# Three slots of 128 partitions in place of four of 72 for the coarse half of attention, in a one-core attention and two-layer kernel

## The chip, the cores and the metric

The kernel runs on one core of a Trainium2 chip. The time is that of the device in microseconds (us), from the start of the program to its end. TensorE multiplies (PE in the rows; its weight loads are PEld), VectorE is DVE, ScalarE is ACT, GpSimd is POOL, and SyncE (SP) issues most transfers. TensorE's results land in eight PSUM banks, and DVE or ACT copies them out.

## The reference

There are 4 batches of 8 heads with 576 positions of 64 numbers. Each head is attended to twice, and the results are added:

```
q_d, k_d, v_d = means of 4 neighbouring positions     # 144 rows each
out_up    = repeat(softmax(q_d k_d^T / 8) v_d, 4)     # the coarse half
out_local = softmax(q k^T / 8 where |i - j| < 4) v    # the local half
x = (out_up + out_local) as 2304 x 512
x = (h * sigmoid(1.702 h)) w_out,  h = x w_in         # layer 1, 512 -> 2048 -> 512
x = elu(h2) w2_out,                h2 = x w2_in       # layer 2
```

The change is in the coarse half alone.

## The kernel before

**Units.** Attention is worked through in units of two heads (head 0 on partitions 0 to 63, head 1 on 64 to 127 of the transposed q and k). There are 16 units: four early ones of batch 0 (whose second half of positions follows in four late ones that have no coarse half of their own), and twelve later ones, "packed", two of which are under way at a time.

**The coarse half of a unit.** `down_products` (step QD) multiplies coarse q by coarse k: the 144 queries of a head are cut into two halves of 72, so there are four slots [72 queries, 144 keys], two for each head, in two PSUM banks. Step ND takes the largest of each row (DVE), NS scales it, EC makes four exps with their sums (ACT, L637), MP weighs them (DVE). `pdt_piece` (PD, L693) turns each slot with two 72x72 transposes, eight in all, into two banks, and PC copies each bank to SBUF (ACT, L701). `pv_down_products` (PVD, L727 and L1023) multiplies them by the coarse v, `vd`, with 72 keys at a time; DN copies the sum. `vd` is made on POOL (L481, L483) from two loads of v (L471), one for each head.

**The local half.** The scores of the windows (QK, L566 and L960), masks, maxima and exps, then `pt_first` and `pt_last` turn the weights (L999, four and one transposes of 128x128), and the products with v (PV, L748 and L1051) follow.

**Shapes on TensorE.** A matmul occupies a part of the 128x128 array that follows from its rows (the contraction) and its columns (the stationary operand's): the layers' matmuls and all the transposes before take 128x128, QD 64x128, PVD 128x64, QK and the packed PV 64x64. In a shape smaller than the array, matmuls on different parts run beside each other: QD's two heads (rows 0 to 63 and 64 to 127), PVD's two heads, four windows in QK and PV. A product of plain float32 shows as two records.

**What sets the order.** Up to the middle of layer 1 a list by hand, `OPENING`, gives the order on all engines, token by token (`QD0.e1`: the coarse products of head 0 of early unit 1; `r` are the packed units). In it stand 40 matmuls on ones (`*10`, `*2`, ...: `keep_busy`) whose results nobody reads. Behind it, a planner cuts each unit into pieces (`pieces`): `attend` is called twice for each step's h (layer 1, first product, L1225) and twice for each step's y (second product, L1292), and takes the next piece once the pause of the one before is over. The pauses are `LEAD` (before the scores, the coarse scores and the turning of q and k) and `BACK` (the pieces behind the exps). TensorE's order is as written; the other engines' follow from it. The last eight units are worked through in this way. Layer 1's loops over the blocks of tokens and layer 2 (L1418, L1467) are as before.

Of the kernel before, what the change touches and what calls it, by code (L numbers as in the profile page):

```python
# [8 lines left out]
F32 = mybir.dt.float32  # L9
# [9 lines left out]
P = 128  # L19
D = 64  # L20
S = 576
SD = 144
HALF = 72
# [37 lines left out]
    Tk0.e1 Tq0.e1 Ck0.e1 VD0.e0 Tk1.e1 Tq1.e1 Ck1.e1 VD0.e2 QD0.e0 Cq0.e1 VD1.e1 Tq0.e3 Sk.e1 QD1.e0 Cq1.e1 LW.2 ND0.e0  # L61
    Cq0.e3 VD0.e1 Tq1.e3 QK.e0 ND1.e0 VD0.e3 Cq1.e3 NS.e0 Sq.e1 VW.e0 EC.e0 NM.e0 *2 QD0.e1 Sq.e3 EW.e0 ND0.e1 *1 QD1.e1
    LQ.r0 Tk0.e3 GA1.e0 ND1.e1 Tk1.e3 Ck0.e3 W.e0 QK.e1 LW.3 NS.e1 Ck1.e3 MS.e0 VD1.e2 EC.e1 Tk0.e2 LK.r0 Sk.e3 NM.e1
    A1.0 MP.e0 *6 QD0.e3 VD1.e3 EW.e1 VW.e1 Tk1.e2 D1.0 D2.0 PT.e0 ND0.e3 QD1.e3 Ck0.e2 PTC.e0 Tq0.e2 Ck1.e2 ND1.e3
    VW.e3 *1 Tq1.e2 A1.1 QK.l0 W.e1 GA0.e0 NS.e3 Cq1.e2 MS.e1 MP.e1 Cq0.e2 PD0.e0 EC.e3 LW.4 *1 QK.e2 LW.5 GA0.e2 NM.l0
    VW.e2 Sq.e2 EW.l0 *2 PD1.e0 QK.e3 NM.e2 LW.6 GA1.e1 PC1.e0 *1 QK.l1 PC0.e0 NM.e3 A3.0 Sk.e2 EW.e2 PD0.e1 PVD.e0 D3.0
    GA0.e1 EW.e3 *2 PV.e0 W.l0 NM.l1 QD0.e2 VW.l0 MS.l0 DN.e0 EW.l1 QD1.e2 W.e3 GA0.e3 X.e0 D1.1 D2.1 VD0.r0 PC0.e1
    MS.e3 *3 Tq0.r0 A3.1 MP.e3 LW.7 PD1.e1 PT.e1 A1.2 GA1.e2 ND0.e2 PD0.e3 XH.00 Cq0.r0 ND1.e2 A1.3 D3.1 *4 Tk0.r0
    PC0.e3 Ck0.r0 NS.e2 XL.00 *1 PTb.l0 GA1.e3 PTC.e1 EC.e2 Tk1.r0 H.0.0 D1.2 D2.2 PTCb.l0 *1 PD1.e3 W.e2 PT.e3 PC1.e1
    D1.3 D2.3 PC1.e3 Tq1.r0 Ck1.r0 PVD.e1 MP.e2 LQ.r1 A3.3 PV.e1 MS.e2 DN.e1 Cq1.r0 PD0.e2 PTC.e3 PT.e2 LW.8 A3.2 X.e1  # L70
    PD1.e2 PC0.e2 PTc.l0 PV.e3 PC1.e2 PTCc.l0 XH.01 W.l1 PVD.e2 A1.4 D3.2 QK.l2 A1.5 PTC.e2 DN.e2 D3.3 *2 PV.e2 XL.01 *1
    H.0.1 X.e2 D1.4 D2.4 PVD.e3 DN.e3 XH.02 MS.l1 *1 PV.l0 X.e3 GA0.r0 XL.02 VW.l1 XH.03 NM.l2 A1.6 H.0.2 VD1.r0 *1 A3.4
# [24 lines left out]
    D3.28 Y.11.0 A1.31 LQ.r4 VD0.r4 A3.30 MP.r3 PVb.r2 H.15.0 Xa.r2 D1.31 GA0.r4 Xb.r2 VD1.r4 GA1.r4 Y.11.1 H.15.1
    PD0.r3 PD1.r3 D3.30 D2.31 Y.12.0 GL.13 ST.14 VD0.r5 MS.r3 PC0.r3 A3.29 PC1.r3 D3.29 TH.15 PTa.r3 PVD.r3 PVa.r3 A3.31
    PTCb.r3 ST.15 DN.r3 GA0.r5 D3.31 PTCa.r3 Y.12.1 GH.15 GL.15 VW.r3 VD1.r5 PVb.r3 GH.14 Xa.r3 GL.14 Xb.r3 GA1.r5
    Y.13.0 Y.13.1 VW.r4  # L100
# [8 lines left out]
BACK = (2, 2, 2)  # L109
# [16 lines left out]
def kernel(  # L126
# [50 lines left out]
    nc.gpsimd.memset(sumset, 1.0)  # L177

# [212 lines left out]
    class Unit:  # L391
# [73 lines left out]
        def load_half(self, j):  # L465
            tag = ("gh", "gl", "gh", "g")[self.hp] if j == 0 else ("gh", "gl", "gl", "g")[self.hp]
            if self in early:
                r = gpool.tile([HALF, 2, 4, D], F32, tag=tag, name=f"vr{j}_{self.n}", bufs=2 if tag == "g" else None)
            else:
                r = att.tile([HALF, 2, 4, D], F32, tag="vr", name=f"vr{j}_{self.n}")  # L470
            nc.sync.dma_start(  # L471
                out=r.rearrange("g c r d -> g c (r d)"),
                in_=v[self.b, 2 * self.hp + j].rearrange("(c g r) d -> g c (r d)", g=HALF, r=4),
            )
            self.halves[j] = r

        def add_half(self, j):
            if self.vd is None:
                self.vd = self.t([HALF, 2, 2, D], "vd", bufs=2)
            r, vd = self.halves.pop(j), self.vd[:, :, j, :]  # L480
            nc.gpsimd.tensor_tensor(out=vd, in0=r[:, :, 0, :], in1=r[:, :, 1, :], op=ALU.add)  # L481
            for i in (2, 3):
                nc.gpsimd.tensor_tensor(out=vd, in0=vd, in1=r[:, :, i, :], op=ALU.add)  # L483
# [111 lines left out]
        def qk_down(self, j):  # L595
            self.down_products(j)
            self.down_max(j)
            if j == 1:
                self.down_scale()

        def down_products(self, j):
            if j == 0:
                self.nmd = self.t([HALF, 4], "nmd", bufs=4)
                self.pd = self.t([HALF, 4, SD], "pd", bufs=2)
                self.psd = {}
            r = slice(64 * j, 64 * j + 64)
            ps = self.ps([HALF, 2, SD], f"qkd{j}")
# [5 lines left out]
            self.psd[j] = ps  # L613

        def down_max(self, j):
            nc.vector.tensor_reduce(
                out=self.nmd[:, 2 * j:2 * j + 2], in_=self.psd[j], axis=AX.X, op=ALU.max, negate=True
            )
# [16 lines left out]
        def exp_down(self):  # L635
            for i in range(4):
                nc.scalar.activation(  # L637
                    out=self.pd[:, i, :], in_=self.psd[i // 2][:, i % 2, :], func=AF.Exp, bias=self.nmd[:, i:i + 1],
                    scale=self.scale_down(), accum_out=self.sums()[:HALF, self.nslot + i:self.nslot + i + 1],
                )  # L640
# [971 lines left out]
```

## Time and profile before

| | |
|---|---|
| median of 3 runs | 917.64 us (916.98 to 923.25) |
| the profiled execution | 917.48 us, of which the span between its first and last instruction is 915.6 us |
| granted TensorE clock | 1.000, the level of 2.4 GHz |
| busy in the span | PE 905.8 us, DVE 463.1 us, ACT 441.4 us, POOL 60.3 us |
| chain that ended last | PE 91%, DVE 3%, ACT 2%, DMA 2%, the rest 2% |

A row of a timeline gives an instruction's start, its duration, and how many like it follow (`x8`); durations of matmuls overlap, so what one costs is the distance between two starts. A row of the groups gives busy time, the mean of one, and the idle time in front with what ended it.

### The profile page before, as it was taken

How to read it: one execution, taken by the hardware profiler on the slowest of the kernel's cores; microseconds unless marked ns; L12 is line 12 of the kernel's file. 1: busy time of each engine (PE TensorE's matmuls, PEld its weight loads, DVE VectorE, ACT ScalarE, POOL GpSimd, SP SyncE). 2: the span in 40 equal slices, each digit the busy share in tenths (PEclk: the TensorE clock that was granted, in tenths of full speed). 3: DMA queues.
4: the chain of work that ended last, by engine and by line, in shares of the span. 5: the costliest groups of instructions: out<-in, count | busy, mean ns of one | idle time of the engine just before them, and what ended most of it. 6: DMA issues, size and time to landing. Idle time of an engine off the chain costs nothing.

```text
span 915.6 us, 14862 instructions
## 1 busy us (share of the span) xinstructions
PE 905.8 (99%) x5823; PEld 747.3 (82%) x5823; DVE 463.1 (51%) x884; ACT 441.4 (48%) x1119; POOL 60.3 (7%) x126
## 2 busy tenths in 40 slices
PE   9999999999999999999999999999999999999998
PEld 5688977777777788888899888778888888888897
DVE  5999888866667532322237765642233223322232
ACT  6888866444446422422246766643334334333343
POOL 4411112111111100000000000000000000000000
PEclk9999999999999999999999999999999999999999
DMA  9997652432233000100069810020001000100010
GB/s 199 217 238 194 189 132 52 102 62 55 54 64 97 23 15 1 47 1 1 0 206 376 292 47 1 0 93 1 1 12 69 1 1 12 46 1 1 7 40 24
DMA packets 113717, 68.05 MB, mean 74 GB/s; under 512 B 81136, under 2 KB 103152, under 8 KB 113648
## 3 DMA queue, kind: packets, MB, share of 16 engines
q1 hardware_dynamic: 111280, 66.52, 26.7%
q10 hardware_dynamic: 2368, 0.59, 0.4%
q8 instruction: 46, 0.75, 0.3%
q14 instruction: 23, 0.19, 0.1%
HBM read 57.65 MB, written 9.44 MB: 73 GB/s over the span
## 4 chain that ended last, share of the span: by engine, by line
PE 91%; DVE 3%; ACT 2%; DMA 2%; SPq 1%; issue 1%; DVEq 0%
PE h L1418 22%; PE o L1467 22%; PE h L1225 18%; PE y L1292 17%; PE y_both L1292 4%; PE h_both L1225 3%; DMA vw<-in_v_dram 1%; PE pv L1051 1%; PE qk L960 1%; PE ptr L999 1%; PE pdt L693 1%; PE qkd L609 1%; SPq L454 1%; DMA rawq<-in_q_dram 1%; PE pv L1023 1%
## 5 line engine op out<-in xcount | busy, mean ns | idle before, releaser
L1467 PE MATMUL o<-whl2o,g2h 128*128 128x512 f32 x576 | 179.7, 392 | 0.0
L1418 PE MATMUL h<-x2h,whl2i 128*128 128x512 f32 (+1 forms) x640 | 158.9, 370 | 0.0
L1292 PE MATMUL y<-g1h,whl1o 128*128 128x512 f32 (+1 forms) x512 | 152.2, 368 | 0.5 <-ACT ye_both L1306 0.5
L1428 DVE SCALAR_TENSOR_TENSOR g<-e,h 128x512 f32<-128x512 f32 (+1 forms) x80 | 50.7, 634 | 196.8 <-ACT e L1426 196.6
L1225 PE MATMUL h<-xh,whl1i 128*128 128x512 f32 (+1 forms) x640 | 145.2, 352 | 0.1
L1418 PEld LDWEIGHTS h<-x2h,whl2i 128*128 128x128 f32 x640 | 114.6, 188 | 22.6
L1467 PEld LDWEIGHTS o<-whl2o,g2h 128*128 128x128 f32 x576 | 106.9, 188 | 24.1 <-DVE whl2o L239 1.2
L1425 ACT ACTIVATE e<-h 128x512 f32<-128x512 f32 (+1 forms) x80 | 44.6, 557 | 164.6 <-PE h L1418 164.4
L1225 PEld LDWEIGHTS h<-xh,whl1i 128*128 128x128 f32 x640 | 105.4, 189 | 15.5 <-issue 0.4
L1467 PE MATMUL o<-whl2o,g2l 128*128 128x512 f32 x288 | 112.6, 391 | 0.0
L1234 ACT ACTIVATE g<-h 128x512 f32<-128x512 f32 x64 | 38.2, 597 | 142.2 <-PE h L1225 141.8
L1292 PEld LDWEIGHTS y<-g1h,whl1o 128*128 128x128 f32 x512 | 92.6, 189 | 17.4 <-issue 1.3
L1238 DVE SCALAR_TENSOR_TENSOR g<-g,h 128x512 f32<-128x512 f32 x64 | 43.9, 686 | 116.7 <-ACT g L1234 116.7
L1292 PE MATMUL y<-g1l,whl1o 128*128 128x512 f32 (+1 forms) x256 | 93.0, 363 | 0.0
L1418 PE MATMUL h<-x2l,whl2i 128*128 128x512 f32 (+1 forms) x320 | 80.0, 371 | 0.0
L1225 PE MATMUL h<-xl,whl1i 128*128 128x512 f32 (+1 forms) x320 | 73.4, 348 | 0.1
L1435 DVE TENSOR_TENSOR g2l<-g,g2h 128x512 fp32r<-128x512 f32 (+1 forms) x80 | 51.0, 638 | 36.8 <-ACT g2h L1433 22.3
L1433 ACT ACTIVATE g2h<-g 128x512 fp32r<-128x512 f32 (+1 forms) x80 | 47.2, 590 | 43.6 <-DVE g L1428 43.6
L1418 PEld LDWEIGHTS h<-x2l,whl2i 128*128 128x128 f32 x320 | 56.8, 188 | 11.0
L1467 PEld LDWEIGHTS o<-whl2o,g2l 128*128 128x128 f32 x288 | 54.1, 188 | 11.6
L1225 PEld LDWEIGHTS h<-xl,whl1i 128*128 128x128 f32 x320 | 54.1, 189 | 8.2 <-DVE xl L384 0.3
L1251 DVE TENSOR_TENSOR g1l<-g,g1h 128x512 fp32r<-128x512 f32 x64 | 44.0, 687 | 30.1 <-ACT g1h L1244 29.7
(142 smaller groups left out, 1170.8 us busy)
## 6 DMA issues: line engine op xcount, KB each, us to landing
wst1i<-in_moe_w_in_dram SPq DMA_DIRECT2D x16, 512.0 KB
wst1o<-in_moe_w_out_dram SPq DMA_DIRECT2D x16, 512.0 KB
wst2o<-in_moe_w_out_dram SPq DMA_DIRECT2D x16, 512.0 KB
wst2i<-in_moe_w_in_dram SPq DMA_DIRECT2D x16, 512.0 KB
vr<-in_v_dram SPq DMA_DIRECT2D x32, 144.0 KB
out_dram<-ot SPq DMA_DIRECT2D x18, 256.0 KB
y<-ydram SPq DMA_DIRECT2D x16, 256.0 KB
ydram<-ye SPq DMA_DIRECT2D x14, 256.0 KB
```

Source lines behind the costliest of these rows:

```text
L454: queue.dma_start(out=r[:, :, j, :], in_=src[self.b, 2 * self.hp + j].rearrange("(p t) d -> p t d", t=6))
L1225: nc.tensor.matmul(out=hps[blk, fs][:, i, :], lhsT=w_in(1, f, c, wp), rhs=columns(xp, c), start=(n == 0), stop=(n >= len(todo) - nf), skip ...
L1234: return nc.scalar.activation(out=g, in_=hps[blk, fs], func=AF.Tanh, scale=0.851)
L1238: return nc.vector.scalar_tensor_tensor(out=g, in0=g, scalar=1.0, in1=ph, op0=ALU.add, op1=ALU.mult)
L1251: return nc.vector.tensor_tensor(out=gl, in0=g, in1=gh.bitcast(F32), op=ALU.subtract)
L1292: nc.tensor.matmul(out=sums(m), lhsT=w_out(1, f, wp)[:, m, :], rhs=gp[:, i, :], start=(opens and n == 0 and m % per == 0), stop=(last and ...
L1418: nc.tensor.matmul(out=ph[:, :n], lhsT=w_in(2, f, c, wp), rhs=xp[:, c, :n], start=(i == 0), stop=(i == 3 * NK - 1),)
L1425: nc.scalar.activation(out=e[:, :n], in_=ph[:, :n], func=AF.Relu, scale=-1.0)
L1428: urgent["dve"] = nc.vector.scalar_tensor_tensor(out=g[:, :n], in0=e[:, :n], scalar=-1.0, in1=ph[:, :n], op0=ALU.add, op1=ALU.max)
L1433: nc.scalar.activation(out=gh[:, :n], in_=g[:, :n], func=AF.Copy)
L1435: return lambda: nc.vector.tensor_tensor(out=gl[:, :n], in0=g[:, :n], in1=gh[:, :n].bitcast(F32), op=ALU.subtract)
L1467: nc.tensor.matmul(out=ops[bi][i], lhsT=gp[:, i * P:(i + 1) * P], rhs=wo[wp], start=(f == 0 and m == 0), stop=(f == NF - 1 and m == 2),)
```

## The change

A unit's coarse half lies in three slots of 128 partitions. Slots 0 and 1 hold queries 0 to 127 of head 0 and head 1; slot 2 holds queries 80 to 143 of head 0 on partitions 0 to 63 and of head 1 on 64 to 127. Queries 80 to 127 are in two slots, and the transposes take them from one. In slot 2, head 1's keys stand with keys 80 to 143 first.

QD is five products (two of 64x128, three of 64x64 with 64 queries each), ND two reductions over three slots, EC three exps, MP one multiplication over 432 numbers in place of 576. PD is one bank: three transposes of 80 queries, one of slot 2's first 128 columns, then one 64x64 transpose for head 0 and, for head 1, one 64x64 product with the identity. PC is one copy of 432 columns. PVD is one product per head over keys 0 to 79 and one for both heads over the last 64 keys of each, whose stationary operand `tails` holds the two heads' tails of v on its diagonal blocks and zeros elsewhere. v is loaded as 80 keys of both heads and, on 128 partitions, a tail; POOL makes seven additions for a unit in place of six, and sets `tails` to zero at the start.

Steps `QD0 QD1`, `ND0 ND1`, `PD0 PD1` and `PC0 PC1` become one each; in `OPENING` they stand mostly where the second of the two stood, with small moves around them. In the planner's last eight units PD joins the turning of the first four pairs (`turned_over`), and `pt_last` moves from there to the front of `pv`, into the second bank of the products. `BACK` has two pauses in place of three.

```diff
-BACK = (2, 2, 2)
+BACK = (2, 2)
...
+    tails = cpool.tile([P, NHP, P], F32, tag="tails", name="tails")
+    nc.gpsimd.memset(tails, 0.0)
...
+            first = self.ps([P, 2, SD], "qkd0")
+            second = self.ps([P, 1, SD], "qkd1")
+            self.psd = first, second
+            every, last = slice(0, SD), slice(KEYS, SD)
+            for out, j, queries, keys in (
+                (first[:, 0, :], 0, slice(0, P), every), (second[:, 0, :], 1, slice(0, P), every),
+                (first[:TAIL, 1, :], 0, last, every), (first[TAIL:, 1, :KEYS], 1, last, slice(TAIL, SD)),
+                (first[TAIL:, 1, KEYS:], 1, last, slice(0, TAIL)),
+            ):
+                r = slice(64 * j, 64 * j + 64)
                 nc.tensor.matmul(
-                    out=ps[:, c, :], lhsT=self.qkd[0][r, c * HALF:(c + 1) * HALF], rhs=self.qkd[1][r, :],
-                    start=True, stop=True,
-                )
+                    out=out, lhsT=self.qkd[0][r, queries], rhs=self.qkd[1][r, keys], start=True, stop=True,
+                    skip_group_check=True,
+                )
...
-            for i in range(4):
+            for i in range(NDOWN):
...
-        def pdt_piece(self, j):
-            if j == 0:
-                self.pdT = self.t([HALF, 4, SD], "pdT")
-            ps = self.ps([HALF, 2, SD], f"pdt{j}")
-            for kc in range(2):
-                for c in range(2):
+        def pdt_piece(self):
+            self.pdT = self.t([P, 3 * SD], "pdT")
+            ps = self.ps([P, 3 * SD], "pdt")
+            pd = self.pd.rearrange("p s k -> p (s k)")
+            for j, k0 in enumerate((0, SD + TAIL, KEYS)):
+                nc.tensor.transpose(
+                    out=ps[:, SD * j:SD * j + KEYS], in_=pd[:KEYS, k0:k0 + P], identity=ident[:KEYS, :KEYS]
+                )
+            nc.tensor.transpose(
+                out=ps[:, :2 * SD].rearrange("p (j q) -> p j q", j=2)[:, :, KEYS:], in_=pd[:, 2 * SD:2 * SD + P],
+                identity=ident,
+            )
+            last = slice(3 * SD - TAIL, 3 * SD)
+            nc.tensor.transpose(out=ps[:TAIL, last], in_=pd[:TAIL, last], identity=ident[:TAIL, :TAIL])
+            nc.tensor.matmul(
+                out=ps[TAIL:, last], lhsT=pd[TAIL:, last], rhs=ident[TAIL:, TAIL:], start=True, stop=True,
+                skip_group_check=True,
+            )
...
+        def pv_down_into(self, ps):
+            for j in range(2):
+                nc.tensor.matmul(
+                    out=ps[64 * j:64 * j + 64, :], lhsT=self.vd[:, j, :], rhs=self.pdT[:KEYS, SD * j:SD * j + SD],
+                    start=True, stop=False, skip_group_check=True,
+                )
+            nc.tensor.matmul(
+                out=ps, lhsT=self.vtail, rhs=self.pdT[:, 2 * SD:], start=False, stop=True, skip_group_check=True
+            )
...
         def turned_over(self):
             while not self.weighed:
                 deferred.pop(0)()
-            last = self.pt_last()
+            down = self.pdt_piece()
             first = self.pt_first()
+            self.pdt_copy(down)
             self.pt_first_copy(first)
-            self.pt_last_copy(last)
...
         def pv(self):
-            down, banks = self.banks_pv()
-            self.pv_down_products(down)
+            down, last, banks = self.banks_pv()
+            self.turn_slots(last.unsqueeze(1), NPAIR - 1, NPAIR)
+            self.pt_last_copy(last)
+            self.pv_down_into(down)
             self.pv_products(banks)
```

TensorE's queue at the coarse scores of one of the planner's units (batch 2, heads 2 and 3), before and then in the change; the shape is the result's:

```order
L1225 MATMUL h_2_3_2831<-xh_2586,whl1i_757 128x512 x4
L609 MATMUL qkd_2_1_0_2853<-kd_1_0_2711,qd_1_0_2709 72x144 x2
L609 MATMUL qkd_2_1_0_2857<-kd_1_0_2711,qd_1_0_2709 72x144 x2
L1292 MATMUL y_2_2786<-g1h_1_2762,whl1o_1050 128x512
```

```order
L1261 MATMUL h_2_3_2803<-xh_2558,whl1i_749 128x512 x4
L642 MATMUL qkd_2_1_0_2825<-kd_1_0_2683,qd_1_0_2681 128x144
L642 MATMUL qkd_2_1_0_2826<-kd_1_0_2683,qd_1_0_2681 128x144
L642 MATMUL qkd_2_1_0_2825<-kd_1_0_2683,qd_1_0_2681 64x144
L642 MATMUL qkd_2_1_0_2825<-kd_1_0_2683,qd_1_0_2681 64x80
L642 MATMUL qkd_2_1_0_2825<-kd_1_0_2683,qd_1_0_2681 64x64
L1328 MATMUL y_2_2758<-g1h_1_2734,whl1o_1037 128x512
```

The two heads' pairs of products became one for each head over 128 queries and three over 64.

TensorE's queue where the first of these units is turned (`pdt`), before and in the change:

```order
L1225 MATMUL h_2_4_2903<-xh_2586,whl1i_905 128x512 x4
L693 MATMUL pdt_2_0_0_2931<-ident,pd_0_0_2680 72x72 x4
L693 MATMUL pdt_2_0_0_2937<-ident,pd_0_0_2680 72x72 x4
L1292 MATMUL y_2_2786<-g1h_2_2782,whl1o_1229 128x512
```

```order
L1261 MATMUL h_2_4_2875<-xh_2558,whl1i_875 128x512 x4
L725 MATMUL pdt_0_0_2903<-ident,pd_0_0_2652 128x80 x3
L728 MATMUL pdt_0_0_2903<-ident,pd_0_0_2652 128x2x64
L733 MATMUL pdt_0_0_2903<-ident,pd_0_0_2652 64x64
L735 MATMUL pdt_0_0_2903<-ident,pd_0_0_2652 64x64
L1042 MATMUL ptr_2_0_0_2911<-ident,sl_0_0_2598 128x128 x4
L1328 MATMUL y_2_2758<-g1h_2_2754,whl1o_1216 128x512
```

The four transposes of the windows' weights (`ptr`) now stand behind the coarse ones, without layer 1's matmuls between.

Its queue at the products with v of the same unit (`PT`, `vw` and `vd` are its operands), before and in the change:

```order
L1292 MATMUL y_2_2789<-g1h_2_2782,whl1o_1229 128x512
L999 MATMUL ptr_2_0_0_2955<-ident,sl_0_0_2626 128x128
L999 MATMUL ptr_2_0_0_2958<-ident,sl_0_0_2626 128x128 x4
L1225 MATMUL h_2_5_2965<-xh_2586,whl1i_946 128x512 x4
L1225 MATMUL h_2_5_2965<-xl_2587,whl1i_946 128x512 x4
L1225 MATMUL h_2_5_2965<-xh_2586,whl1i_946 128x512 x4
L1023 MATMUL pv_2_0_0_2985<-pdT_0_0_2930,vd_0_0_2431 64x144 x4
L1051 MATMUL pv_2_0_0_2985<-PT_0_0_2957,vw_0_0_2576 64x60
L1051 MATMUL pv_2_0_0_2986<-PT_0_0_2957,vw_0_0_2576 64x57
```

```order
L1328 MATMUL y_2_2761<-g1h_2_2754,whl1o_1216 128x512
L1042 MATMUL pv_2_0_0_2931<-ident,sl_0_0_2598 128x128
L769 MATMUL pv_2_0_0_2930<-pdT_0_0_2902,vd_0_0_2406 64x144 x2
L773 MATMUL pv_2_0_0_2930<-pdT_0_0_2902,tails 128x144
L1085 MATMUL pv_2_0_0_2930<-PT_0_0_2910,vw_0_0_2548 64x60
L1085 MATMUL pv_2_0_0_2931<-PT_0_0_2910,vw_0_0_2548 64x57
L1085 MATMUL pv_2_0_0_2930<-PT_0_0_2910,vw_0_0_2548 64x60
```

The last transpose stood twelve matmuls of layer 1 ahead of the products; now nothing of layer 1 stands between, and `pv_2_0_0_2931`, into which it goes, is the bank of every second product.

ScalarE's queue around the copy of that transpose (`PT`), before and in the change:

```order
L1234 ACTIVATE g_2_4_2923<-h_2_4_2903 128x512
L701 ACTIVATE pdT_0_0_2930<-pdt_2_0_0_2931 72x288
L701 ACTIVATE pdT_0_0_2930<-pdt_2_0_0_2937 72x288
L1244 ACTIVATE g1h_4_2926<-g_2_4_2923 128x512
L1018 ACTIVATE PT_0_0_2957<-ptr_2_0_0_2955 128x128
L1234 ACTIVATE g_2_5_2978<-h_2_5_2965 128x512
L1244 ACTIVATE g1h_5_2981<-g_2_5_2978 128x512
```

```order
L1270 ACTIVATE g_2_4_2895<-h_2_4_2875 128x512
L742 ACTIVATE pdT_0_0_2902<-pdt_0_0_2903 128x432
L1280 ACTIVATE g1h_4_2898<-g_2_4_2895 128x512
L1061 ACTIVATE PT_0_0_2910<-pv_2_0_0_2931 128x128
L780 ACTIVATE dn_0_0_2957<-pv_2_0_0_2930 128x144
L1270 ACTIVATE g_2_5_2997<-h_2_5_2984 128x512
```

Two copies of the coarse transposes became one; the copy of the last pair stands behind the same `g1h`.

## Rows read from the trace of the kernel before

**Rows 1.** The page: busy us of each engine, share of the span, instructions.

```profile
PE 905.8 (99%) x5823; PEld 747.3 (82%) x5823; DVE 463.1 (51%) x884; ACT 441.4 (48%) x1119; POOL 60.3 (7%) x126
```

**Rows 2.** Waits of TensorE: who waited for whom, us in total, times, longest.

```profile
PE pdt L693 <- ACT whl1i L235: 0.7, 2, 0.4
PE pdt L693 <- DVE pd L672: 0.7, 1, 0.7
...
PE pdt L693 <- ACT pdT L701: 0.3, 1, 0.3
```

**Rows 3.** Stretches: length, busy us PE, PEld, DVE, ACT, POOL; clock, DMA share, GB/s.

```profile
12.00:45.00 33.00, 31.36 (x380) 22.64 (x381) 30.06 (x69) 30.15 (x122) 13.96 (x24) 1.00 1.02 219
45.00:100.00 55.00, 53.68 (x562) 48.66 (x558) 52.76 (x116) 43.58 (x128) 7.59 (x12) 1.00 0.85 221
206.00:332.00 126.00, 126.00 (x1057) 99.80 (x1057) 75.96 (x163) 60.96 (x238) 13.67 (x30) 1.00 0.26 56
```

**Rows 4.** Timeline of PE at a unit's coarse scores.

```profile
204.94 1.07 PE L1225 MATMUL h<-xh,whl1i 128*128 128x512 f32 x4
205.94 0.72 PE L609 MATMUL qkd<-kd,qd 64*72 64x144 f32 x8
206.59 0.50 PE L1292 MATMUL y<-g1h,whl1o 128*128 128x512 f32 x1
206.93 0.40 PE L1292 MATMUL y<-g1l,whl1o 128*128 128x512 f32 x1
```

**Rows 5.** Timeline of PE at a unit's coarse transposes.

```profile
275.12 0.40 PE L1292 MATMUL y<-g1h,whl1o 128*128 128x512 f32 x1
275.35 0.66 PE L693 MATMUL pdt<-ident,pd 72*72 72x72 f32 x8
275.82 0.48 PE L1292 MATMUL y<-g1h,whl1o 128*128 128x512 f32 x1
276.14 0.39 PE L1292 MATMUL y<-g1l,whl1o 128*128 128x512 f32 x1
```

**Rows 6.** Timeline of PE at a unit's products with v.

```profile
303.12 0.71 PE L1023 MATMUL pv<-pdT,vd 72*64 72x144 f32 x8
303.76 0.91 PE L1051 MATMUL pv<-PT,vw 64*64 64x60 f32 x40
```

**Rows 7.** Timeline of PE at the first early unit.

```profile
10.96 0.71 PE L609 MATMUL qkd<-kd,qd 64*72 64x144 f32 x4
11.60 0.47 PE L513 MATMUL pt<-ident,rawq 96*128 96x96 f32 x3
12.00 0.71 PE L609 MATMUL qkd<-kd,qd 64*72 64x144 f32 x4
12.64 0.47 PE L513 MATMUL pt<-ident,rawq 96*128 96x96 f32 x3
...
13.15 0.71 PE L566 MATMUL qk<-kT,qT 64*64 64x70 f32 x16
```

**Rows 8.** Groups of all PE's instructions, by form.

```profile
L693 PE MATMUL pdt<-ident,pd 72*72 72x72 f32 x128 | 11.6, 227 | 1.6 <-ACT whl1i L235 0.7 <-DVE pd L672 0.7 <-ACT pdT L701 0.3
...
L999 PE MATMUL ptr<-ident,sl 128*128 128x128 f32 x60 | 9.0, 274 | 0.0
```

**Rows 9.** Groups of ACT's instructions, by form.

```profile
L637 ACT ACTIVATE pd<-qkd,nmd 72x144 f32<-72x144 f32 x64 | 23.2, 379 | 6.7 <-DVE nmd L621 6.7
...
L701 ACT ACTIVATE pdT<-pdt 72x288 f32<-72x288 f32 x32 | 11.8, 416 | 5.4 <-PE pdt L693 5.4
```

**Rows 10.** Timeline of ACT at the planner's first unit.

```profile
212.43 0.60 ACT L1234 ACTIVATE g<-h 128x512 f32<-128x512 f32 x1 [0.44 <-PE h L1225]
...
214.63 0.63 ACT L1244 ACTIVATE g1h<-g 128x512 fp32r<-128x512 f32 x1 [1.01 <-DVE g L1238]
215.79 0.28 ACT L1018 ACTIVATE PT<-ptr 128x128 f32<-128x128 f32 x1 [0.52 <-PE ptr L999]
```

More of the change, by code (lines that the diff above doesn't have):

```diff
@@ L22 @@
 SD = 144
-HALF = 72
+KEYS = 80
+TAIL = 64
+NDOWN = 3
 NWIN = 9
@@ L469, in load_half @@
             else:
[L470 to L473, printed above, removed]
-            )
[L475 to L483, printed above, removed]
+                r = att.tile([P, 2, 4, D], F32, tag="vr", name=f"vr{part}_{self.n}")
@@ new lines, in load_half, with add_half @@
+            self.halves[part] = r
+        def add_half(self, part):
+            r = self.halves.pop(part)
+            if part == 0:
+                self.vd = self.t([KEYS, 2, D], "vd", bufs=2)
+                nc.gpsimd.tensor_tensor(out=self.vd, in0=r[:KEYS, :, 0, :], in1=r[:KEYS, :, 1, :], op=ALU.add)
+                for i in (2, 3):
+                    nc.gpsimd.tensor_tensor(out=self.vd, in0=self.vd, in1=r[:KEYS, :, i, :], op=ALU.add)
+                return
+            t = r[:, 0]
+            for i in (1, 2):
+                nc.gpsimd.tensor_tensor(out=t[:, 0], in0=t[:, 0], in1=t[:, i], op=ALU.add)
+            self.vtail = tails[:, whole.index(self) % NHP]
+            for j in range(2):
+                rows = slice(TAIL * j, TAIL * j + TAIL)
+                nc.gpsimd.tensor_tensor(out=self.vtail[rows, rows], in0=t[rows, 0], in1=t[rows, 3], op=ALU.add)
@@ L808, in one @@
                 self.exp_windows(*{"": qk_at[""], "a": (0, 3), "b": (3, 6), "c": (6, NWIN)}[part])
[L809 to L816 removed]
+            elif step == "PD":
+                ps["pd"] = self.pdt_piece()
+            elif step == "PC":
+                self.pdt_copy(ps.pop("pd"))
             elif kind == "PT":
@@ L948, in banks_pv @@
             first = self.ps([P, n + SD], "pv0")
-            second = self.ps([P, 87, 4], "pv1")
-            return first[:, n:], [first[:, :n].rearrange("p (g r) -> p g r", r=4), second]
+            second = self.ps([P, n + P], "pv1")
+            return first[:, n:], second[:, n:], [t[:, :n].rearrange("p (g r) -> p g r", r=4) for t in (first, second)]
         def qk_products(self):
@@ L1018, in pt_last_copy @@
             nc.scalar.activation(out=self.PT[:, NPAIR - 1], in_=ps[:, :P], func=AF.Copy)
-        def pv_down_products(self, ps):
-            for kc in range(2):
-                for j in range(2):
-                    nc.tensor.matmul(
-                        out=ps[64 * j:64 * j + 64, :], lhsT=self.vd[:, kc, j, :],
-                        rhs=self.pdT[:, 2 * j + kc, :], start=(kc == 0), stop=(kc == 1), skip_group_check=True,
-                    )
-            return ps
         def turned_over(self):
```

179 lines of the change are left out of this document (83 added, 96 removed).

## The prediction

> **What bounds the kernel now.** I read the page first: TensorE is busy for 905.8 of 915.6 us, the others for half of it or less [rows 1]. Then TensorE's own waits: they are few and short, those at the coarse transposes come to 1.7 us [rows 2]. Then the stretches: from 206 us on, where the planner works, TensorE is busy all the time, while DVE is at 60% and ACT at 48%; before that, from 12 to 45 us, all three are near full, ACT for 30.15 and DVE for 30.06 of 33 us [rows 3]. So the time is the length of TensorE's queue, and an instruction less on ACT or DVE is worth only the wait of TensorE that it ends, in the opening alone. In the opening the matmuls on ones stand in the queue as before; they are not shortened by anything that the change does. The question is what the new pieces cost on TensorE, so I went on to its timeline around each step.
>
> **Prices.** One of the layers' matmuls of 512 columns follows the next after 0.23 us (275.12 to 275.35, [rows 5]). Eight transposes of 72 columns last 0.66, the last of them 0.23 [rows 5, 8], so they begin 0.062 apart: 0.86 ns a column. That makes 0.123 for a pass of 144 columns, 0.110 for 128, 0.069 for 80, 0.055 for 64. A plain product has two passes, its two records.
>
> A change of shape costs more than any of these. At the coarse scores the last of the four h matmuls began at 204.94 + 1.07 - 0.39 = 205.62; QD follows 0.32 later, 0.09 over the 0.23; QD's four passes (the two heads beside each other) are 0.49, and the next matmul begins 0.65 after it, 0.16 over; the one behind comes after 0.34, 0.11 over [rows 4]. Going in and coming out is 0.36 together. Between two small shapes, PVD's 128x64 and PV's 64x64, it is 0.64 - 0.49 = 0.15 [rows 6]. So I count 0.15 for a change, and 0.21 where a matmul of 512 follows it. Standing between the layers' matmuls without a change of shape costs 0.07: from 275.12 to 276.14 there are 1.02, less two times 0.23, less 0.49 for the eight transposes [rows 5].
>
> **The change, part by part.**
>
> *Coarse scores.* Two products over 128 queries beside each other are 2 x 0.123; then the array goes from 64x128 to 64x64, where head 0 has 2 x 0.123 and head 1 beside it 2 x (0.069 + 0.055). The passes are 0.49 as before, and there is one more change of shape: +0.15 in each of the twelve packed units, 1.8. In three of the four early units the two halves stood apart, each of 0.64 (10.96 to 11.60 and 12.00 to 12.64) with its own way in and out [rows 7]; put together they lose four passes that nothing ran beside, 0.49, and one way in and out, 0.30 between short transposes, and gain 0.15: -0.64 each, -1.9. The fourth has +0.15. Together 0.0.
>
> *Coarse transposes.* Before eight of 0.062, 0.49, in the layers' own shape. Now 3 x 0.069 + 0.110 + two passes of 0.055 for the product with the identity, with the 64x64 transpose beside it: 0.43, and two changes of shape. In the eight units that the opening turns that is -0.06 + 0.15 + 0.21 = +0.30, 2.4 in all. In the planner's eight the windows' transposes follow, so it is -0.06 + 0.15 + 0.15, less 0.07 for one interruption fewer: +0.17, 1.4 in all. What no row shows is a transpose of 128 stationary and 80 moving columns: if it took as long as one of 128 moving, it would be 0.041 more, 2.0 over 48 of them. I take the moving columns, by which the row of 72 goes, and keep 2.0 for the upper end.
>
> *Products with the coarse v.* Two heads beside each other over 80 keys, 2 x 0.123, and one product over the tails, 2 x 0.123: 0.49 as before. The tails' product is 128x128. In the planner's units the 64x64 products follow, one change more, 8 x 0.15 = 1.2; in the four packed units of the opening the way out becomes a way within, 4 x -0.06 = -0.2; in the early ones nothing. Together +1.0.
>
> *ACT and DVE.* A unit has one exp less, 0.38, and one copy of 432 columns for two of 0.416; between 0.42 (288 columns) and 0.63 (512) I take 0.56 [rows 9, 10]. That is 0.65 us of ACT for each unit, and a quarter of DVE's maxima and weighing. From 206 us on it is worth nothing, since both wait for TensorE there. In the opening it can end waits at the coarse transposes; I take off half of their 1.7, 0.8. At worst, with all of the second PD's work now due before the first turn, they grow by as much.
>
> *The rest.* Seven additions for six on POOL, and the zeros of `tails` at the start, lie in POOL's idle time: it works 13.67 of 126 us where the planner runs, and 7.59 of 55 in the opening [rows 3]; without that cover a unit would pay one addition, 0.46 (13.67 over 30). Transfers are as many, in other cuts. `BACK` with two pauses ends attention earlier, and TensorE has the same work whenever it comes; in that stretch DVE goes from 60% to some 70%.
>
> Sum: 0.0 + 3.8 + 1.0 - 0.8 = +4.0. The profiled execution took 917.48, of which 915.6 are span; the median of the runs is 917.64, the same within 0.02%. **Forecast: 921.5 us**, 919 to 924.5 by itself. By this kernel's runs, a difference under 1%, 9.2 us, is what I call no change.
>
> **Rivals.**
>
> *New pairs of shapes that share a side cost nothing* (64x128 to 64x64, 128x64 to 128x128). For it: no row has just these pairs. Against it: 128x64 to 64x64 share a side too, and cost 0.15 [rows 6]. It takes off 16 x 0.15 and 8 x 0.15: 917.9. Chance 0.10.
>
> *The opening is set by ACT and DVE, and passes their relief on.* For it: they are 91% busy from 12 to 45 us [rows 3]. Against it: TensorE waits there for next to nothing [rows 2], and the matmuls on ones stay. The opening's eight units give up to 8 x 0.65 = 5.2 on ACT; if TensorE's waits and slack give 4 of it, less the 0.8 that I counted: 918.3, and with luck below the time before. Chance 0.17.
>
> *The copy of the last pair holds the products.* In the planner's units every second product with v goes into the bank that ACT must first have read. From the start of the transpose TensorE has 0.110 + 0.15 + 0.25 + 0.15 + 0.25 + 0.15 = 1.06 us of its own work; the transpose lasts 0.27 [rows 8] and the copy 0.28 [rows 10], so the copy may begin some 0.5 late. Behind one tanh or one `g1h` (0.60 and 0.63 [rows 10]) it is late by 0.1 at the most; behind both, by 0.7. If that held in all eight units: 921.5 + 5.6 = 927.1, and with the dear transposes 929. It decides where ACT is over 0.5 us behind TensorE; against it, ACT had been idle for 0.52 before that copy [rows 10]. Chance 0.10.
>
> *The two halves of a bank are written one after the other.* The 16 products of an early unit's scores go in pairs, from both row halves into one bank; singly they would be 16 passes of 70 columns, 0.96, and they last 0.71 with the end of the last [rows 7]: the pairs run beside each other. The Trainium skill, page "TensorEngine Tiling (Array Packing)", section "Gotcha 1: PSUM Pressure", says that different row tiles cannot be in the same PSUM bank at the same time; the trace does not bear that out for different partitions. If it held for the new pieces (head 1's 0.25 at the scores and 0.055 at the transposes, which share a bank with head 0's), it would add 16 x 0.30 = 4.9: 926.4. Chance 0.04.
>
> **How the numbers follow.** The forecast has 0.55, the rivals 0.10, 0.17, 0.10 and 0.04, and 0.04 are left for what I do not see. The range goes from 916, with the first two rivals taken together in part, to 927.5, with the dear transposes or the copies in most units. Under 908.3 nothing above leads: 0.02. Over 926.8 there are the copies, half of the bank rival, and the rest: 0.12. Between them 0.86.
>
> **What would show it.** In the changed profile: TensorE busy all the time from 206 us to the end of attention; the stretch between a PD's first transpose and the matmul behind it longer by 0.3; a coarse score group of 0.80 between its start and the next matmul, in place of 0.65; the three transposes 0.07 apart, not 0.11; the copy of the last pair over before the products with v begin. I am wrong on the low side if the waits of the opening shrink by several us or the changes of shape within QD show no gap, and on the high side if TensorE waits for ACT at the products with v.

## The result: slower by 1.3%, and the profile after

The changed kernel takes 929.37 us (median of 7 runs, 927.52 to 934.43), the kernel before 917.49 beside it (7 runs): 1.0127 times as long, 95% interval 1.0100 to 1.0153. The forecast was 921.5, its range ended at 927.5. The profiled execution took 928.87 (span 927.2); where a difference below comes from traces, it is against the 915.6 of the profile before.

The waits of TensorE in the changed kernel (who waited for whom, us in total, times, longest), as [rows 2] show them before:

```profile
PE qk L583 <- ACT qs L551: 1.1, 1, 1.1
PE ptr L752 <- ACT qT L551: 0.7, 2, 0.5
PE qkd L642 <- DVE kd L555: 0.7, 1, 0.7
...
PE pt L539 <- ACT pd L668: 0.6, 1, 0.6
...
PE pvd L769 <- DVE sumset L699: 0.5, 1, 0.5
```

The waits at the coarse transposes are gone, as forecast. Others stand in their place, at the windows' scores, the turning of q and k, and the products with the coarse v. The stretches of [rows 3] now (same columns):

```profile
12.00:45.00 33.00, 29.35 (x334) 20.03 (x330) 27.09 (x66) 28.64 (x110) 14.15 (x29) 0.99 0.94 226
45.00:100.00 55.00, 53.34 (x573) 47.61 (x570) 50.25 (x113) 41.21 (x114) 5.90 (x14) 0.97 0.70 197
206.00:332.00 126.00, 125.86 (x1067) 97.94 (x1067) 74.70 (x167) 57.69 (x218) 15.08 (x38) 1.00 0.27 58
```

From 206 to 332 us TensorE is busy all the time but for 0.14 us (before, all the time). Between 12 and 45 us all three engines do less than before (PE 29.35 for 31.36, ACT 28.64 for 30.15, DVE 27.09 for 30.06): ACT and DVE have less work there, and TensorE waits more. And the clock is no longer 1.00. In pieces of 2 us:

```profile
40.00:42.00 2.00, 2.00 (x28) 1.52 (x25) 0.42 (x1) 1.37 (x4) 0.00 (x0) 1.00 0.89 199
42.00:44.00 2.00, 1.07 (x8) 0.56 (x7) 1.89 (x6) 1.97 (x5) 0.00 (x0) 1.00 0.98 271
44.00:46.00 2.00, 2.00 (x23) 1.05 (x22) 0.76 (x2) 0.11 (x1) 1.83 (x3) 0.63 1.09 240
46.00:48.00 2.00, 2.00 (x21) 1.81 (x21) 0.73 (x2) 0.00 (x0) 0.13 (x1) 0.52 0.45 139
48.00:50.00 2.00, 2.00 (x28) 1.46 (x26) 1.16 (x3) 0.60 (x2) 1.16 (x3) 1.00 0.00 1
```

TensorE was busy for 1.07 of the 2 us from 42; then it was granted its lower level (1.2 GHz) until some 47.9.

TensorE's timeline at one of the planner's units: scores, transposes, products (as [rows 4], [rows 5], [rows 6]):

```profile
190.55 0.92 PE L642 MATMUL qkd<-kd,qd 64*128 64x144 f32 x10
191.40 0.50 PE L1328 MATMUL y<-g1h,whl1o 128*128 128x512 f32 x1
...
216.06 0.37 PE L725 MATMUL pdt<-ident,pd 80*128 80x80 f32 x3
216.27 0.27 PE L728 MATMUL pdt<-ident,pd 128*128 128x128 f32 x1
216.47 0.24 PE L733 MATMUL pdt<-ident,pd 64*64 64x64 f32 x1
216.65 0.32 PE L735 MATMUL pdt<-ident,pd 64*64 64x64 f32 x2
216.90 0.66 PE L1042 MATMUL ptr<-ident,sl 128*128 128x128 f32 x4
217.31 0.71 PE L1261 MATMUL h<-xh,whl1i 128*128 128x512 f32 x2
...
220.15 0.27 PE L1042 MATMUL pv<-ident,sl 128*128 128x128 f32 x1
220.52 0.47 PE L769 MATMUL pv<-pdT,vd 80*64 80x144 f32 x4
220.92 0.51 PE L773 MATMUL pv<-pdT,tails 128*128 128x144 f32 x2
221.36 0.91 PE L1085 MATMUL pv<-PT,vw 64*64 64x60 f32 x40
```

Read the starts, since ends overlap. The scores take 0.85 from start to the next matmul, not 0.65. The three transposes are 0.07 apart, as forecast. The 128-column transpose and its way out take 0.20; then the 64x64 transpose starts 0.17 *before* the product on the other tile: here they do not run beside each other. PVD takes 0.84 in place of 0.64.

**Where it went.** I added up, over TensorE's records, the time from each start to the next start, by kind of piece; "layers" are the 512-column matmuls, PT the transposes of pairs. The planner's stretch, from the 625th to the 1170th of the layers' matmuls (8 units; 7 scores groups), in us:

```
                before   changed   e3_shapes
QD (7)            4.56      5.92      5.92
PD (8)            3.73      6.74      5.40
PT (8)            3.70      5.18      5.44
PVD (8)           5.13      6.71      5.14
layers          130.47    128.88    128.90
all             158.78    164.61    161.98
```

With the eighth scores group the planner costs 6.0. The same layer matmul starts 5.5 us later than before where the opening ends (the one at 174.8 us before) and 11.5 later where the planner ends (338.7 us before); from there it stays 11.5. So there are two halves, and the experiments go by them.

### The profile page after: what moved, and what is told of

It reads as the page before. It is cut to its first block, busy times and chain, and to the rows that moved or that the text cites. A ratio compares the mean times of both kernels' runs of the same rounds, so it can differ in the third digit from the quotient of the medians.

```text
span 927.2 us, 14801 instructions
## 1 busy us (share of the span) xinstructions
PE 915.4 (99%) x5807; PEld 752.3 (81%) x5807; DVE 454.8 (49%) x884; ACT 433.7 (47%) x1071; POOL 59.9 (6%) x143
## 4 chain that ended last, share of the span: by engine, by line
PE 91%; DMA 2%; DVE 2%; SPq 2%; ACT 2%; issue 1%; DVEq 0%; ACTq 0%
PE h L1454 22%; PE o L1503 21%; PE h L1261 17%; PE y L1328 17%; PE y_both L1328 4%; PE h_both L1261 3%; DMA vr<-in_v_dram 2%; PE pv L1085 1%; PE qkd L642 1%; PE qk L1003 1%; PE ptr L1042 1%; SPq L458 1%; ACT sl L661 0%; PE pv L793 0%; SPq L199 0%
## 5 line engine op out<-in xcount | busy, mean ns | idle before, releaser
L1503 PEld LDWEIGHTS o<-whl2o,g2l 128*128 128x128 f32 x288 | 54.1, 188 | 11.5
```

The source lines that it names most:

```text
L1503: nc.tensor.matmul(out=ops[bi][i], lhsT=gp[:, i * P:(i + 1) * P], rhs=wo[wp], start=(f == 0 and m == 0), stop=(f == NF - 1 and m == 2),)
```

## The experiments

**e1_planner_four and e2_opening_four: the two halves apart.** Units of both kinds in one kernel, by class:

```diff
-    rest = [Packed(b, hp) for b in range(1, B) for hp in range(NHP)]
+    rest = [(Packed if b == 1 else Packed4)(b, hp) for b in range(1, B) for hp in range(NHP)]   # e1
+    rest = [(Packed4 if b == 1 else Packed)(b, hp) for b in range(1, B) for hp in range(NHP)]   # e2, and
+    early = [Unit4(0, hp, 0, 4) for hp in range(NHP)]                  # e2, with the list of before
```

> The eight units that the planner runs have four slots of 72 again, with their three pieces (2, 2, 2); the opening keeps the three slots of 128 and its list. Theory: the loss is made in two separate halves. In the changed kernel the layers' first matmuls stand 5.5 us behind those of the kernel before where the opening ends and 11.5 us where the planner ends, so the planner's units cost 6.0 (0.75 each) on TensorE by themselves; without them 929.4 - 6.0 = 923.4 (922.4 to 924.4). Rival: the planner's stretch only pays for what the opening left late; then 928 to 929.5.

> The reverse: the eight units of the opening have four slots, in the order of the kernel before; the planner's eight units have three. Theory of two halves: 917.5 + 6.0 = 923.5 (922.5 to 924.5), the granted clock at 1.00 throughout, the early layer matmuls where they were before within 0.5 us. Rival (the planner's loss is inherited from the opening): 917.5 to 919.

e2: 922.83 us (10 runs; 1.0061 of the kernel before, 1.0040 to 1.0082), inside the expectation. Its layer matmuls stand 0.7 us ahead of before's where the opening ends and 5.25 behind where the planner ends: the planner alone costs 5.9. e1: 922.01, 923.11, 928.73 and 928.74, mean clocks 0.999, 0.997, 0.991 and 0.991. At near full clock it is at the lower end of the expectation or just below it; its median (925.92) is above it. In its trace the layers' matmuls are 4.39 late at both ends of the planner, so four slots there add nothing. Two separate halves: shown. No trace is kept of the two executions that lost more of the clock. But e1 has nothing of the change behind 175 us, and in every kept trace the granted clock, where it falls before the program's last 2 us, is low only between 21 and 56 us (the traces of the changed kernel, e3, e4, e5, e8 and e9): the loss of the clock belongs to the opening.

**e3_shapes: the new pieces in cheaper shapes.**

```diff
-            nc.tensor.transpose(out=ps[:TAIL, last], in_=pd[:TAIL, last], identity=ident[:TAIL, :TAIL])
+            nc.tensor.matmul(out=ps[:TAIL, last], lhsT=pd[:TAIL, last], rhs=ident[:TAIL, :TAIL], ...)
...
-            nc.tensor.matmul(out=ps, lhsT=self.vtail, rhs=self.pdT[:, 2 * SD:], ...)
+            for j in range(2):
+                nc.tensor.matmul(out=ps[64 * j:64 * j + 64, :], lhsT=self.vtail[:, 64 * j:64 * j + 64],
+                                 rhs=self.pdT[:, 2 * SD:], ...)
```

> The changed kernel with two edits on TensorE and none in its order: head 0's last 64x64 piece of the coarse transposes is a plain product with the identity, as head 1's is, and the product over the tails is two of 128x64 in place of one of 128x128. Theory: a change of array shape costs the end of the pass under way (0.095) and the first weight load behind it (0.05 for 64 columns, 0.10 for 128), and the 64x64 transpose and product do not run beside each other (0.17 from one to the other). Then the coarse transposes are 0.12 to 0.17 shorter in 16 units (1.9 to 2.8), and the products with the coarse v 0.20 in the planner's 8 units and 0.10 to 0.20 in the opening's 8 (2.4 to 3.2): 929.4 - 4.3 to 6.0, so 924.3 (923.4 to 925.1). Rival: the two products stay one after the other because they write one bank, and the tails' two products too: 929 +- 1.

923.59 us (7 runs), 5.8 less than the changed kernel, inside the expectation. TensorE's timeline at the same pieces:

```profile
216.92 0.37 PE L725 MATMUL pdt<-ident,pd 80*128 80x80 f32 x3
217.13 0.27 PE L728 MATMUL pdt<-ident,pd 128*128 128x128 f32 x1
217.33 0.27 PE L733 MATMUL pdt<-ident,pd 64*64 64x64 f32 x1
217.34 0.27 PE L738 MATMUL pdt<-ident,pd 64*64 64x64 f32 x1
217.44 0.22 PE L733 MATMUL pdt<-ident,pd 64*64 64x64 f32 x1
217.44 0.22 PE L738 MATMUL pdt<-ident,pd 64*64 64x64 f32 x1
217.59 0.66 PE L1047 MATMUL ptr<-ident,sl 128*128 128x128 f32 x4
...
221.32 0.47 PE L772 MATMUL pv<-pdT,vd 80*64 80x144 f32 x4 [0.20 <-DVE PT L1058]
221.59 0.45 PE L777 MATMUL pv<-pdT,tails 128*64 128x144 f32 x4
221.97 0.91 PE L1090 MATMUL pv<-PT,vw 64*64 64x60 f32 x40
```

Two plain products on two tiles start 0.01 apart and are through in 0.26, where transpose and product took 0.43: one record more, 0.17 less. They come from different row halves and write one bank, so the bank rival is out. The tails in two products of PVD's own shape bring PVD back to 0.65. In the planner PD falls by 1.34 and PVD by 1.57, PT gains 0.26 (PVD now waits 0.20 for a copy on DVE): 2.6 in all. The other 3 us came in the opening. A part of it may be the clock: three of its seven runs had a mean clock of 1.000, of the changed kernel's seven one. Between the traces of e6_fill and e11_shapes_fill below, which differ by the same two edits and are both at 1.000, the opening gains 1.6.

**e4_order: the changed list's further moves undone.** The list of before, with each merged step at its second half's place; e.g.

```diff
-PVD.e0 D3.0 GA0.e1 EW.e3 *2 W.l0 NM.l1 MS.l0 DN.e0 PV.e0 VW.l0 EW.l1 QD.e2
+PVD.e0 D3.0 GA0.e1 EW.e3 *2 PV.e0 W.l0 NM.l1 VW.l0 MS.l0 DN.e0 EW.l1 QD.e2
```

> The changed kernel with the opening's list as the kernel before has it, each merged step at the place of its second half, instead of the changed list's further moves (products with v behind the coarse copy, score steps later); one products step, PV of the fourth early unit, must stand four steps later, right behind PVD of the third. Theory: a part of the opening's 5.5 us are waits that those further moves made; TensorE waits less at 20 to 22 us and 42 to 44 us, the granted clock stays at 1.00 at 44 to 48 us, and the time is 926 to 928. Rival: the waits come from the merged pieces, which bring all of a unit's work to one place; then they only change places, 929 +- 1, with the clock lower in some stretch again.

930.41 us (4 runs, 927.95 to 932.26): the rival's side, and just above its 930. At a mean clock of 1.000 it took 927.95, the changed kernel 927.52. So undoing the further moves gains nothing; that theory fell, and the merged steps themselves came under suspicion.

**e5_four_merged, e9_merge_scores, e10_scores_apart: merged steps.** e5 and e9 have no new shape, e10 has all of them.

```diff
-            if step[:2] == "QD":
-                self.down_products(int(step[2]))
+            if step in ("QD", "ND", "PD", "PC"):      # e5: all four, with the changed list; e9: QD and ND alone
+                for j in range(2):
+                    ...
+            elif step in ("QD0", "QD1"):              # e10, three slots: slots 0 and 2, then slot 1
+                self.down_part(int(step[2]))
```

> All sixteen units have the four slots of 72 again, and the planner runs its eight as before (2, 2, 2); but the opening follows the changed kernel's list, in which both halves of a unit's coarse scores, maxima, transposes and copies are one step each. No new array shape is left, ACT has four exps and two copies again. Theory: of the 4.5 us that the opening lost at full clock in the planner-four run, some 2.4 arose before 62 us as new waits, because a merged step takes two PSUM banks at once and everything it needs must be there; then 917.4 + 2 to 3.5 = 919.4 to 921, and TensorE waits over 0.5 us at the scores after 20 us again. Rival: the opening lost it by the array shapes of the new pieces alone; then 917 to 918.5, since two early pieces in one save their way in and out.

922.36 us (10 runs; 1.0061, 1.0037 to 1.0085), above the expectation, and 920.11, inside it, in its one run at a mean clock of 1.000. So merging alone costs, without a new shape. It overstates: four merged slots take two banks at the transposes, where three take one, and the longest wait of its trace (an execution at a mean clock of 0.988) is there:

```profile
PE pdt L1239 <- ACT qT L564: 2.5, 1, 2.5
...
PE qk L596 <- ACT qs L564: 1.0, 1, 1.0
```

The scores alone take two banks in either kernel, hence e9.

> The kernel before in slots, planner and list, but the two halves of a unit's coarse score products, and of their maxima, are one step at the place of the second half. Theory: in the opening the merged scores take two PSUM banks at one moment and bring the maxima, exps and all behind them together, so TensorE waits at 20 to 22 us and later; it saves 0.63 in each of three units on TensorE and still is no faster: 917.5 to 919.5. Rival: the waits of the run with all steps merged came from its transposes alone (two banks for one); then the saved 1.9 us show: 915.3 to 917.

917.94 us (10 runs; 1.0006, 0.9991 to 1.0020). TensorE's scores of the early units fell from 4.86 to 3.41 us (sum to the 60th layer matmul; 0.66 of the 3.41 is idle time behind them, so the pieces themselves gave 2.1), and the time did not fall. The waits of its trace, an execution at a mean clock of 0.996:

```profile
PE qk L597 <- ACT qs L565: 1.1, 1, 1.1
PE pdt L1240 <- DVE pd L717: 0.8, 1, 0.8
PE pt L553 <- DVE sumset L1224: 0.7, 1, 0.7
```

The first is that of the changed kernel, at the same scores, which wait for a copy on ACT. TensorE's timeline at that place in the changed kernel:

```profile
20.61 0.47 PE L539 MATMUL pt<-ident,rawq 96*128 96x96 f32 x3
22.13 0.31 PE L583 MATMUL qk<-mask,identb 128*128 128x350 bf16 x1 [1.05 <-ACT qs L551]
22.37 0.83 PE L592 MATMUL qk<-kT,qT 64*64 64x70 f32 x20
```

Before, these scores began 0.24 behind the last of the turns and waited for nothing:

```profile
21.40 0.41 PE L513 MATMUL pt<-ident,rawq 96*128 96x96 f32 x3
21.64 0.31 PE L557 MATMUL qk<-mask,identb 128*128 128x350 bf16 x1
```

> The changed kernel with the early units' coarse scores in two steps again (slots 0 and 2, then slot 1) at the places that the kernel before has for its halves; all else as changed. On TensorE that costs about 0.43 in each of three units, 1.3 in all. Theory: the merged scores cause most of the opening's new waits; without them 927.5 + 1.3 - 2 to 3, 926 to 927, with the clock at 1.00. Rival: the waits come from the merged transposes and the moved products; then only the 1.3 show, and the clock is lost as in the changed kernel: 929 to 931.

928.36 us (4 runs, all at 0.999 or 1.000): between the two expectations. The wait at 21 us is gone, the clock is kept, and TensorE pays 1.5 more for the scores than in e6_fill, which has them merged and takes 0.4 less. Merged or apart is one price here: what TensorE saves, it then waits, in the main. So at full clock the merged scores neither win nor lose; they may put the clock at risk (e9's runs: 0.996 to 1.000, the kernel before beside them 0.998 to 1.000).

**e6_fill: the clock alone.** Five matmuls on ones in the changed list:

```diff
-PTC.e2 PVD.e2 QK.l2 DN.e2
+PTC.e2 *2 PVD.e2 *3 QK.l2 DN.e2
```

> The changed kernel with five more matmuls on ones where TensorE waited just before its clock fell: two ahead of the third early unit's products with the coarse v (a wait of 0.47), three ahead of the scores behind them (0.75). Theory: the granted clock at 44 to 48 us was lost by these waits and cost some 1.5 us; with them filled it stays at 1.00 in most runs and the median falls from 929.4 to that of the changed kernel's one run at full clock, 927.5 (927 to 928.2). Rival: the clock is lost by the waits at 20 to 22 and 33 to 36 us, or for another reason: 929 to 930.5.

927.94 us (4 runs, 927.64 to 929.00, mean clocks 0.998 to 1.000), 1.4 less than the changed kernel, from few runs whose ranges overlap. The same stretches:

```profile
42.00:44.00 2.00, 1.91 (x13) 1.03 (x13) 1.51 (x5) 1.77 (x4) 0.70 (x1) 1.00 0.77 238
44.00:46.00 2.00, 2.00 (x33) 1.15 (x33) 1.14 (x3) 0.50 (x2) 1.91 (x2) 1.00 0.88 214
46.00:48.00 2.00, 2.00 (x29) 1.60 (x24) 1.42 (x4) 0.00 (x0) 0.00 (x0) 1.00 0.90 290
```

TensorE busy for 1.91 for 1.07, and the clock stays at its higher level behind it. But the waits of that place do not decide it alone. In e10_scores_apart, without these matmuls on ones, TensorE was as little busy, and the clock stayed:

```profile
42.00:44.00 2.00, 1.08 (x7) 0.56 (x7) 1.76 (x6) 1.99 (x5) 0.00 (x0) 1.00 0.59 141
44.00:46.00 2.00, 1.99 (x39) 1.31 (x38) 0.89 (x2) 0.24 (x2) 1.61 (x3) 1.00 0.99 309
```

So a group of waits puts the clock at risk and does not always cost it. With the fill, six of eight executions have a mean clock of 1.000 (e6, e11 below); without it four of fourteen (the changed kernel, e3). That work that computes nothing made the kernel faster is likely by this, and not shown beyond it.

**e7_before_pieces: the planner's merged pieces with four slots.** BACK (2, 2), PD in `turned_over`, the last pair's transpose in `pv`.

> The kernel before, four slots, with only the planner's new arrangement: the coarse transposes and the first four transposes of pairs are one piece, the last pair's transpose opens the piece of the products, pieces (2, 2). Theory: an interruption of the layers' matmuls less in eight units, 0.07 each, and earlier by one pause; TensorE is busy throughout: 917.4 - 0.6 = 916.8 (916.2 to 917.4). Rival: the products with v now wait for the copy of the last pair on ACT, 0.2 to 0.7 in each unit: 919 to 922.

925.94 us (4 runs; 1.0088, 1.0067 to 1.0110), slower than both expectations, and not by the rival's wait but by another:

```profile
PE ptr L999 <- ACT pdT L701: 6.2, 8, 2.6
```

Four slots' transposes fill two banks, so the pairs' transposes behind them must wait for a copy. So it does not tell what the new arrangement alone is worth; it shows that the planner's merged piece stands on the three slots' transposes fitting one bank.

**e8_act_back: ACT's relief given back.**

```diff
+            if self in whole[:2 * NHP]:
+                nc.scalar.activation(out=spare_exp, in_=self.psd[1][:, 0, :], func=AF.Exp, ...)
```

> The changed kernel with one exp of 144 columns more in each of the opening's eight units, its result unused: ACT gets back the 0.38 that the change took from each of its softmaxes, 3.0 in all. Theory: ACT's relief is worth nothing, because TensorE's own order and its waits for single results set the end and ACT stands idle for half of 36 to 48 us: 929.4, 928.5 to 930.3. Rival: the relief is passed on by about half, as the prediction had it in part: 930.5 to 932.

929.63 us (4 runs, 928.43 to 931.58), as the changed kernel by the median. At a mean clock of 1.000 its two runs took 928.43 and 928.57, the changed kernel's one 927.52. So 3 us of exps added in the opening cost between nothing and some 1 us.

**e11_shapes_fill and e12_merge_fill: what can be had.** e3 with e6's five matmuls, and e9 with `*5` ahead of `QK.l0`.

> The three slots as cheap as these runs make them: head 0's last piece as a plain product, the tails in two products of 128x64, and the five matmuls on ones ahead of the third early unit's products and scores. Expected as the sum of the two runs: the two edits gave 5.8 from median to median, of which 2.7 in the planner; the fill keeps the clock at 1.00: 922 to 923.3, still above the 917.5 of the kernel before, since the planner's units keep 0.4 each and the opening its waits.

> The four slots with merged early scores (the run that stood level with the kernel before), and five matmuls on ones where TensorE then waits 1.3 us, ahead of the first late unit's scores. Theory: the clock, which that run lost in most of its executions at 22 to 30 us, is kept, so its median goes from 917.9 to that of its executions at full clock, 915.9 to 917.6: 916.5, level with the kernel before or 0.1% faster. Rival: the merged scores' waits, not the clock, hold it: 917.5 to 918.5.

e11: 923.37 us (4 runs; 1.0073, 1.0058 to 1.0088), just above the expectation. The fill gives next to nothing more on the median of e3 (923.59); three slots stay 6 us slower. e12: 917.52 (12 runs; 1.0001, 0.9992 to 1.0011), its clock kept at 0.998 to 1.000. That is the rival's number: with the clock kept, the merged scores are still no faster than the kernel before, which nothing here beats.

## Why the prediction was wrong

The mechanism, that TensorE's queue sets the time and new shapes lengthen it, was right. Two terms were too small, and a third was missing. The time went over the forecast by 7.9 us: 2.2 of it in the planner, 4.2 in the opening and 1.4 with the clock. Of the 11.9 us between 917.49 and 929.37:

- **The planner: forecast +3.8, measured +6.0.** I priced each change of shape at 0.15, from [rows 4] and [rows 6]. The scores grew by 0.19 a unit (QD 5.92 for 4.56 over 7), PVD by 0.20. The first pass behind a change lasts 0.227 where 128 stationary columns are loaded (the scores, the tails) and 0.180 where 72 are (the scores before), over the same 144 moving ones. In PVD's own shape the tails' four records take 0.38, in the new one two take 0.44. The Trainium skill, page "TensorE: Matmul & The Clock Gate", section "LDWEIGHTS (loading the stationary operand)", says that a weight load lasts by its columns; the trace agrees in direction. At the transposes, **the step that failed is "the 64x64 transpose beside" the product**: it ran ahead of it, 0.17 in each of 16 units (why, no run shows). I had taken what two plain products do (the early scores' pairs, [rows 7]) for a transpose and a product. And I overlooked that the pairs' transposes change neighbours: PT grew by 1.48 in all, the first behind the 64x64 pieces and the last one with the way into PVD. The interruption fewer gave 1.59 at the layers' matmuls, 0.20 a unit, where I had 0.07. PD, PT and layers together: +2.9 for +1.4.
- **The opening at full clock: forecast about +0.2, measured +4.4** (e6_fill against before, where the opening ends; e1's trace gives 4.4 too). One trace of the opening is good to about 1 us: e2 and e7, which have the opening of the kernel before, stand 0.7 and 1.0 ahead of its trace there. Sums to the 60th layer matmul and from there to the 625th: PD 4.38 to 6.74, the forecast 2.4, met in part by luck, since in the opening the two halves stood apart before and cost 0.65 more than in the planner; PVD 5.03 to 5.87, where I had -0.2, since the tails' product stands in all eight units; QD 8.11 to 7.83, where I had -1.2. That is +2.9 for +1.0. The rest, some 1.5, goes with waits: TensorE's idle time up to the 625th layer matmul grew from 4.7 to 6.7 us. **Here the step that failed is "I take off half of their 1.7, 0.8"**: those waits went, and more came elsewhere. I saw that TensorE would wait less at the coarse transposes, but not what is late next: merged scores bring a unit's maxima, exps and weighing together, and what stands behind them waits for ACT and DVE (e9, e10). ACT's relief, in the forecast as half of 1.7 us and in a rival as 4, was not worth it: an exp of 0.38 added back in each of the eight units cost 1 us at the most (e8).
- **The clock: not in the forecast, some 1.4 us.** Six of seven executions have a mean clock under 1.000; in the profiled one the lower level came behind the new waits at 42 to 44 us, and e6_fill, which fills them, mostly kept the higher one. That these waits alone decide it is not shown (e10 kept the clock with them). I priced each wait by its length; I should have asked what a cluster of them does to the work behind it.

The rivals: the copy of the last pair does not hold the products (in the unit shown it ended at 221.18, and they began at 221.36); the only wait found there is one of 0.20 for the other copy, in e3. The bank rival is out by e3's products. That new pairs of shapes cost nothing, or that the opening passes relief on, is out by the above. What held: TensorE busy from 206 to 332 us, three transposes 0.07 apart, coarse pieces longer though not by how much. The last condition named for the high side, TensorE waiting for ACT at the products with v, did not occur; the time went over by other ways.

By e9 and e10 the waits go, in the main, with the merged scores: apart, the scores cost TensorE 1.5 more and the opening is no longer. What the merged transposes do to the waits by themselves stays open: e5's take two banks, the changed kernel's one, and no run merges the transposes alone.

## What to carry to other kernels

On a kernel that TensorE bounds, count shapes before instructions: 0.15 to 0.2 us for each change of array shape, the more where the stationary operand behind it has 128 columns (a first pass of 0.227, against 0.180 with 72), and keep a group's pieces in the shape of their neighbours, even at one matmul more. Merging two steps of a hand-made order saves TensorE's ways in and out, but takes banks and makes results due together; price the wait of whatever stood between them. Where TensorE's waits come in a cluster, look at the granted clock behind it: a few matmuls that compute nothing may pay (some 1.4 us in e6, nothing in e12).

## What the runs showed of the hardware beyond that

A transpose and a plain product on diagonal 64x64 tiles ran one after the other (0.17), two plain products beside each other (0.01 apart) into one bank from different row halves. The Trainium skill, page "TensorEngine Tiling (Array Packing)", section "Key Properties", says that a change of tiling mode drains TensorE, which these rows bear out: 0.20 for the 128-column transpose ahead of a change, where four of its like take 0.41, the way in included (216.90 to 217.31). It says there too that different tiles can load and multiply in parallel; the two plain products agree, and for a transpose beside a product no run here shows that.

The same stretch of waits, TensorE busy for 1.07 and 1.08 of 2 us, was followed by the lower clock level in one execution (the changed kernel) and by the higher in another (e10).
